# Loading wq in four strided quarters, x behind a tiny Exp, and a no-operation that waits for the last loads

## Chip, cores, metric

One core of a Trainium2 chip. The time is device time in microseconds (us) of one execution. Some executions here are about 1.2 to 1.6 us longer; they are called "slow" and left out of ratios. A ratio is the mean time of one kernel's fast runs over the mean of the other's fast runs of the same rounds on the same chip, so it is not quite the ratio of the medians that are quoted.

## The reference

A decode step for one token. `q = x @ wq` has 32 heads of 128; they attend to the last 4096 positions of 8 K/V heads, and the result goes through `wo`. Beside it stands a gated unit on the same x. A sigmoid gate mixes the two.

```python
q = (x @ wq).reshape(B, Sq, Hq, Dh).transpose(0, 2, 1, 3)      # x 1x512, wq 512x4096
k, v = k_cache[:, :, Sk - W:], v_cache[:, :, Sk - W:]           # 8 heads, W = 4096, Dh = 128
o = softmax(q @ k.T * Dh ** -0.5) @ v                           # k, v repeated over 4 heads each
a = o.reshape(B, Sq, Hq * Dh) @ wo                              # wo 4096x512
b = (sigmoid(x @ w_gate) * (x @ w_up)) @ w_down                 # F = 1792
g = sigmoid((x * gate_w).sum(-1, keepdims=True))
return g * a + (1 - g) * b
```

All of it is 30.67 MB of bf16 read once: a kernel of transfers.

## The kernel before

All large loads are issued by SyncE, in the order in which they are used, into tiles that are there from the start or come free on the way.

```python
const = ctx.enter_context(tc.tile_pool(name="const", bufs=1))
big = ctx.enter_context(tc.tile_pool(name="big", bufs=1))
blk = ctx.enter_context(tc.tile_pool(name="blk", bufs=4))
w14 = ctx.enter_context(tc.tile_pool(name="w14", bufs=3))
# ... cut: further pools
xr = const.tile([1, 2, D], BF16, name="xr")
nc.scalar.dma_start(xr[:, 0, :], A_x[0, :, :])
nc.scalar.dma_start(xr[:, 1, :], gate_w.rearrange("(o n) -> o n", o=1))

dq = nc.sync
wq_sb = big.tile([P, DC, HQ * DH], BF16, name="wq_sb", tag="big")
wq_v = A_wq.rearrange("(p c) n -> p c n", c=DC)      # 32 KB in a row for each of 128 partitions
dq.dma_start(wq_sb[:], wq_v)
# ... cut: K in 4 loads, w_gate, w_up (wx: a part of it, in 4 small loads), V in 4, wo in 2, w_down in 4
spare = const.tile([1, 1], F32, name="spare")
for _ in range(4):
    nc.vector.memset(spare[:], 0.0)
# ... cut: identities, x transposed by TensorE, the gate
for k in range(8):                                    # q: needs all partitions of wq
    # ... cut
    for c in range(DC):
        nc.tensor.matmul(q_ps[:], lhsT=xT[:, c:c + 1].to_broadcast([P, P]),
                         rhs=wq_sb[:, c, ks], start=(c == 0), stop=(c == DC - 1))
# ... cut: K transposed by VectorE, scores, softmax, V, gated unit, wo and w_down into a_ps, output
```

## Time and profile before

| | before |
|---|---|
| median of the first 3 runs (range) | 80.73 us (80.44 to 81.89) |
| span in the profile | 78.7 us |
| first packet of wq starts | 1.74 us |
| wq complete | 12.93 us |
| last piece of w_down complete | 75.84 us |
| output issued | 76.68 us |

"Complete" is the last increment of a load's semaphore, from the trace's records of increments; packets are from its records of DMA packets.

### The profile page before, as it was taken

How to read it: one execution, taken by the hardware profiler on the slowest of the kernel's cores; microseconds unless marked ns; L12 is line 12 of the kernel's file. 1: busy time of each engine (PE TensorE's matmuls, PEld its weight loads, DVE VectorE, ACT ScalarE, POOL GpSimd, SP SyncE). 2: the span in 40 equal slices, each digit the busy share in tenths (PEclk: the TensorE clock that was granted, in tenths of full speed). 3: DMA queues.
4: the chain of work that ended last, by engine and by line, in shares of the span. 5: the costliest groups of instructions: out<-in, count | busy, mean ns of one | idle time of the engine just before them, and what ended most of it. 6: DMA issues, size and time to landing. Idle time of an engine off the chain costs nothing.

```text
span 78.7 us, 798 instructions
## 1 busy us (share of the span) xinstructions
PE 52.5 (67%) x314; PEld 23.6 (30%) x314; DVE 38.8 (49%) x52; ACT 10.9 (14%) x20; POOL 3.3 (4%) x10
## 2 busy tenths in 40 slices
PE   0200094999905788898887307999996799567650
PEld 0200041344302333333332202344341345345420
DVE  1600920029869999999986349962000000690020
ACT  2400000247651000000002191000000002000010
POOL 7900000000000000000000000000000000000000
PEclk9999999999999999999999995699999999999997
DMA  7779799999999999999999999999999999999710
GB/s 184 300 316 533 316 483 391 408 425 458 441 408 416 425 474 416 386 437 417 438 410 426 441 416 441 408 433 441 416 433 433 424 425 433 416 391 409 290 42 1
DMA packets 2616, 30.71 MB, mean 390 GB/s; under 512 B 307, under 2 KB 438, under 8 KB 822
## 3 DMA queue, kind: packets, MB, share of 16 engines
q1 hardware_dynamic: 2608, 30.67, 92.9%
q8 instruction: 2, 0.03, 0.2%
q10 hardware_dynamic: 6, 0.00, 0.0%
HBM read 30.67 MB, written 0.00 MB: 390 GB/s over the span
## 4 chain that ended last, share of the span: by engine, by line
DMA 93%; SPq 2%; PE 1%; DVE 1%; issue 0%
DMA wd_sb<-in_B_w_down_dram 36%; DMA kn<-in_A_k_cache_dram 32%; DMA vv<-in_A_v_cache_dram 24%; SPq L84 2%; PE a_ps L290 1%; DVE res L341 1%; SPq L80 0%
## 5 line engine op out<-in xcount | busy, mean ns | idle before, releaser
L299 PE MATMUL pv_ps<-vv,eT 128*32 128x512 bf16 x64 | 15.9, 405 | 4.1 <-DVE eT L271 2.8
L227 PE MATMUL S_ps<-kT,qbig 128*128 128x512 bf16 x64 | 15.2, 378 | 5.0 <-DVE qbig L216 2.8
L188 DVE STREAM_TRANSPOSE kT<-kn 128x2048 f32<-128x2048 f32 x8 | 17.8, 2282 | 0.0
L227 PEld LDWEIGHTS <-qbig 128*128 128x128 bf16 x64 | 6.1, 97 | 14.1 <-issue 4.2
L299 PEld LDWEIGHTS <-eT 128*32 128x32 bf16 x64 | 6.2, 102 | 12.9 <-issue 4.2
L200 PE MATMUL q_ps<-wq_sb,xT 128*128 128x512 bf16 x32 | 8.8, 442 | 1.2 <-DMA wq_sb<-in_A_wq_dram 1.2
L318 DVE TENSOR_TENSOR oT<-o_ps,rb 128x32 bf16<-128x32 f32 x1 | 0.2, 191 | 13.5 <-PE o_ps L316 13.5
L205 DVE STREAM_TRANSPOSE qtT<-q_sb 128x512 f32<-128x512 f32 x4 | 2.7, 700 | 6.9 <-ACT q_sb L202 6.9
L182 PE MATMUL S_ps<-ident,other 2*128 2x512 bf16 x4 | 2.0, 611 | 5.8 <-DVE other L140 5.8
L202 ACT CAST q_sb<-q_ps 128x512 bf16<-128x512 f32 x8 | 4.7, 585 | 7.0 <-PE q_ps L200 7.0
L200 PEld LDWEIGHTS <-xT 128*128 128x128 bf16 x32 | 3.5, 111 | 6.8 <-issue 4.2
L290 PE MATMUL a_ps<-wo_sb,oY 128*1 128x256 bf16 x64 | 3.8, 272 | 1.5 <-DMA wo_sb<-in_A_wo_dram 1.2
L290 PEld LDWEIGHTS <-oY 128*1 128x1 bf16 x64 | 2.7, 83 | 3.1 <-issue 1.4
L271 DVE STREAM_TRANSPOSE eT<-e_sb 128x1024 bf16<-128x1024 bf16 x2 | 2.4, 1224 | 1.9 <-ACT e_sb L269 1.9
L254 ACT ACTIVATE sge<-gu_ps 128x448 f32<-128x448 f32 x1 | 0.5, 543 | 18.9 <-PE gu_ps L243 18.9
L309 ACT COPY pv_sb<-pv_ps 128x512 f32<-128x512 f32 x1 | 0.6, 585 | 17.7 <-PE pv_ps L299 17.7
L341 DVE CAST res<-a_ps 1x256 bf16<-1x256 f32 x1 | 0.4, 412 | 5.2 <-PE a_ps L290 5.2
L281 DVE RECIPROCAL sg<-sge 128x448 f32<-128x448 f32 x1 | 3.0, 2952 | 0.0
L165 DVE TENSOR_TENSOR gpr<-xr 1x512 f32<-1x512 bf16 x1 | 0.7, 679 | 4.6 <-DMA xr<-in_gate_w_dram 4.6
L249 DVE TENSOR_REDUCE pm<-S_ps 128x1 f32<-128x1024 f32 x2 | 2.4, 1208 | 0.9 <-PE S_ps L227 0.9
L290 PE MATMUL a_ps<-wd_sb,hT 128*1 128x256 bf16 x28 | 2.1, 271 | 0.8 <-DMA wd_sb<-in_B_w_down_dram 0.8
L148 PE MATMUL xt_ps<-ident,xr 1*128 1x1 bf16 x4 | 0.3, 165 | 3.5 <-POOL ident L126 3.5
(62 smaller groups left out, 31.0 us busy)
## 6 DMA issues: line engine op xcount, KB each, us to landing
kn<-in_A_k_cache_dram SPq DMA_DIRECT2D x4, 2048.0 KB, 27.2
vv<-in_A_v_cache_dram SPq DMA_DIRECT2D x4, 2048.0 KB, 19.1
wq_sb<-in_A_wq_dram SPq DMA_DIRECT2D x1, 4096.0 KB
wo_sb<-in_A_wo_dram SPq DMA_DIRECT2D x2, 2048.0 KB
wg_sb<-in_B_w_gate_dram SPq DMA_DIRECT2D x1, 1792.0 KB
wu_sb<-in_B_w_up_dram SPq DMA_DIRECT2D x1, 1456.0 KB
wd_sb<-in_B_w_down_dram SPq DMA_DIRECT2D x1, 1024.0 KB
wd_sb<-in_B_w_down_dram SPq DMA_DIRECT2D x1, 384.0 KB
```

The source lines that it names most:

```text
L84: dq.dma_start(t[:, n0:n1, :].rearrange("p n d -> p (n d)"), cache[0, 2 * a:2 * a + 2, SBASE:SBASE + W, :] .rearrange("y (x n) d -> x y n ...
L182: nc.tensor.matmul(S_ps[u // 2][:, u % 2, :], lhsT=other[:].rearrange("p o y u -> p (o y u)"), rhs=ident[0:2, 0:2].rearrange("p (o y) -> p ...
L188: nc.vector.transpose(t[:].bitcast(F32), kn[a][:, v * KB:(v + 1) * KB, :] .rearrange("p n d -> p (n d)").bitcast(F32))
L200: nc.tensor.matmul(q_ps[:], lhsT=xT[:, c:c + 1].to_broadcast([P, P]), rhs=wq_sb[:, c, ks], start=(c == 0), stop=(c == DC - 1))
L202: nc.scalar.copy(q_sb[:, ks], q_ps[:])
L205: nc.vector.transpose(qtT[:].bitcast(F32)[:, kq], q_sb[:].bitcast(F32)[:, kq])
L227: nc.tensor.matmul(S_ps[v][:, hb, :], lhsT=q_st[:, a, dhi, :, t], rhs=k_v[:, hb * 16:(hb + 1) * 16, dhi, :, t], start=False, stop=(a == HP ...
L249: nc.vector.tensor_reduce(pm2[:, v:v + 1], S_ps[v][:].rearrange("p a b -> p (a b)"), axis=AX.X, op=ALU.max)
L271: nc.vector.transpose(eT[:, :, v * KB:(v + 1) * KB, :].rearrange("p a n r -> p n a r"), e_sb[:, v, :].rearrange("p (n a r) -> p n a r", a= ...
L281: nc.vector.reciprocal(sg[:], sge[:])
L290: nc.tensor.matmul(a_ps[32 * i:32 * i + 1, i, 0:HN], lhsT=lhsT, rhs=rhs[:, i * HN:(i + 1) * HN], start=start, stop=stop)
L299: nc.tensor.matmul(pv_ps[32 * a:32 * a + 32, :, :], lhsT=eT[:, a, 4 * m:4 * m + 4, :].rearrange("p n r -> p (n r)"), rhs=vv[a][:, 4 * m:4 ...
```

## The change

The intent, as the diff lets one guess: to give wq the first place in the queues, to split it so that its first part is under way sooner while each part still touches every fourth partition, to fetch ScalarE's table early, and to have SyncE's waits for the loads done before the end.

```diff
+    ctx.enter_context(tc.manual_schedule(engines={mybir.EngineType.Activation}))
+    warm = const.tile([1, 1], F32, name="warm")
+    nc.vector.memset(warm[:], 0.0)
+    nc.scalar.activation(warm[:], warm[:], AF.Exp)
     xr = const.tile([1, 2, D], BF16, name="xr")
@@
-    dq.dma_start(wq_sb[:], wq_v)
+    for y in range(4):
+        dq.dma_start(wq_sb[y:P:4], wq_v[y:P:4])
@@ (the loads of K, V, wo and w_down are also kept in a list, loads)
+    seen = dq.nop()
+    for load in loads[-8:]:
+        tc.add_manual_dep(seen.ins, load.ins.name,
+                          mybir.DependencyInfo(mybir.DependencyClass.Sync, mybir.DependencyReason.DATA), reason="loads ended")
@@
-    for _ in range(4):
+    for _ in range(3):
         nc.vector.memset(spare[:], 0.0)
```

More of the change, by code (lines that the diff above doesn't have):

```diff
@@ L77 @@
     dq = nc.sync
+    loads = []
     wq_sb = big.tile([P, DC, HQ * DH], BF16, name="wq_sb", tag="big")
     wq_v = A_wq.rearrange("(p c) n -> p c n", c=DC)
-    dq.dma_start(wq_sb[:], wq_v)
+    for y in range(4):
+        dq.dma_start(wq_sb[y:P:4], wq_v[y:P:4])
     def load_pair(t, cache, a, n0=0, n1=NP):
-        dq.dma_start(t[:, n0:n1, :].rearrange("p n d -> p (n d)"),
-                     cache[0, 2 * a:2 * a + 2, SBASE:SBASE + W, :]
-                     .rearrange("y (x n) d -> x y n d", n=NP)[:, :, n0:n1, :].rearrange("x y n d -> x y (n d)"))
+        loads.append(dq.dma_start(t[:, n0:n1, :].rearrange("p n d -> p (n d)"),
+                                  cache[0, 2 * a:2 * a + 2, SBASE:SBASE + W, :]
+                                  .rearrange("y (x n) d -> x y n d", n=NP)[:, :, n0:n1, :].rearrange("x y n d -> x y (n d)")))
     kn = []
@@ L114 @@
     for c0 in (0, NC_O // 2):
-        dq.dma_start(wo_sb[:, c0:c0 + NC_O // 2, :], wo_v[:, c0:c0 + NC_O // 2, :])
+        loads.append(dq.dma_start(wo_sb[:, c0:c0 + NC_O // 2, :], wo_v[:, c0:c0 + NC_O // 2, :]))
     wd_sb = w14.tile([P, NJ, N_OUT], BF16, name="wd_sb", tag="w14")
@@ L119 @@
     for j0, j1 in zip(WD_SPLIT[:-1], WD_SPLIT[1:]):
-        dq.dma_start(wd_sb[:, j0:j1, :], wd_v[:, j0:j1, :])
+        loads.append(dq.dma_start(wd_sb[:, j0:j1, :], wd_v[:, j0:j1, :]))
+    seen = dq.nop()
+    for load in loads[-8:]:
+        tc.add_manual_dep(seen.ins, load.ins.name,
+                          mybir.DependencyInfo(mybir.DependencyClass.Sync, mybir.DependencyReason.DATA), reason="loads ended")
     identf = const.tile([P, P], F32, name="identf")
```

## The prediction

> **What bounds the kernel now.** I read the chain that ended last first, in order of time; its columns are start, duration, what.
>
> ```profile
> 2.52 25.10 DMA kn<-in_A_k_cache_dram
> ...
> 27.70 19.12 DMA vv<-in_A_v_cache_dram
> ...
> 46.84 28.67 DMA wd_sb<-in_B_w_down_dram
> 75.51 0.04 issue
> 75.55 0.66 PE a_ps L290 x6
> 76.20 0.40 DVE res L341
> ```
>
> From 2.5 to 75.5 us it is transfers only; compute adds about 1.1 us behind the last one. Then I asked whether the DMA queue ever runs dry, with the 40 slices and the queue table of the page (packets, MB, share of 16 engines):
>
> ```profile
> DMA  7779799999999999999999999999999999999710
> ...
> q1 hardware_dynamic: 2608, 30.67, 92.9%
> ```
>
> It is full from the fifth slice to the end, and only the first four slices (8 us) are ragged. The packet records of the trace say the same in detail: in the steady part a 32 KB packet takes 1.23 us on its DMA engine, so 16 engines move 16 x 32768 B / 1.23 us = 426 GB/s. 30.67 MB at that rate are 72.0 us. Transfers run from 1.74 us (first packet of wq) to 75.84 us (last increment of the last piece of w_down), 74.1 us. So all that could be won without moving fewer bytes is about 2.1 us, and it has two places. (a) The first packets of wq start between 1.74 and 2.55 us, end between 3.60 and 4.09 us, and take 1.4 to 2.15 us in place of 1.23. (b) At the end the 16 engines are not level: of the last load six increments come at 74.1 to 74.3 us, ten at 75.5 to 75.8 us. The change touches (a) alone.
>
> The start, from the timeline of the first 20 us (start, duration, engine, line; in brackets the idle time before and what ended it):
>
> ```profile
> 0.73 0.38 SPq L80 DMA_DIRECT2D wq_sb<-in_A_wq_dram  x1
> 0.74 0.51 ACTq L74 DMA_DIRECT2D xr<-in_A_x_dram  x1
> ...
> 1.28 0.21 ACTq L75 DMA_DIRECT2D xr<-in_gate_w_dram  x1
> ...
> 1.53 1.28 ACT L170 ACT_TABLE_LOAD   x1 [1.53 <-PEq L358]
> ...
> 7.83 0.68 DVE L165 TENSOR_TENSOR gpr<-xr 1x512 f32<-1x512 bf16 x1 [4.56 <-DMA xr<-in_gate_w_dram]
> ...
> 12.98 7.25 PE L200 MATMUL q_ps<-wq_sb,xT 128*128 128x512 bf16 x25 [1.17 <-DMA wq_sb<-in_A_wq_dram]
> ```
>
> The reader is to see that x and wq are issued at the same instant from two queues; that gate_w, issued 0.5 us later, is not usable before 7.8 us; and that the q matmuls wait for all of wq, until 12.98 us. Last, the slack of compute, from TensorE's timeline near the end:
>
> ```profile
> 61.58 2.97 PE L299 MATMUL pv_ps<-vv,eT 128*32 128x512 bf16 x13 [1.28 <-DMA vv<-in_A_v_cache_dram]
> ...
> 71.38 1.91 PE L290 MATMUL a_ps<-wo_sb,oY 128*1 128x256 bf16 x32 [1.22 <-DMA wo_sb<-in_A_wo_dram]
> ```
>
> TensorE waits 1.28 us for V and then 1.22 us for wo, then 0.61 and 0.19 us for w_down. Work that reaches TensorE up to about 1.28 + 1.22 = 2.5 us later than now still ends behind the same transfers.
>
> [...]
>
> **The change part by part.**
>
> *wq in four loads.* Same bytes, same 32 KB rows, eight packets per engine. SyncE pays four issues for one. An issue of 128 rows takes 0.38 us here, one of a single row 0.21 us, so I take 0.3 us for 32 rows, an estimate: about 1.2 us in place of 0.38, and the first K load is issued some 0.8 us later. That lies far ahead of need, since wq alone keeps the engines busy until 12.6 us. The eight completion semaphores are handed out in turn, so with three more loads the third K load must wait for the first quarter of wq, and the fourth for x; both come long before 12 us, while four to six MB are queued. Cost on the path: 0. The gain: in the old single load packets began over 0.8 us and none ended before 3.60. [...] The last of the old packets to begin still took 1.54 us, 0.31 over the steady 1.23, so of the mean excess (about 1.9 - 1.23 = 0.7 us) some 0.4 us can go. Every engine then ends 0.4 us earlier.
>
> *x and gate_w behind the Exp.* No instruction of ScalarE's arithmetic is saved on the path: the table load is in both kernels, and it was idle time before (the Exp that needs it runs at 10.5 us). The tiny Exp is about 0.2 us of an idle engine. Its purpose can only be to leave wq the first place. x is then issued at 1.0 us if the queue runs on beside the table load, at about 2.1 us if not. Behind wq's packets it will wait as gate_w does now: a landing at 6 to 8.5 us in place of 2.0, and gate_w at 8 to 11 in place of 7.8. VectorE does gpr, gsum, two small operations and xT after gate_w, 9.69 - 7.83 = about 1.9 us, and TensorE the four mask matmuls, 2.1 us. So q could begin at 13 to 15.2 us in place of 12.98, a delay of 0 to 2.2 us. VectorE's chain to the exponentials shifts by as much, and the slack of 2.5 us less the 0.4 us gained takes it up. Cost on the path: 0, probably.
>
> *The no-operation.* It is one wait more on a queue that has nothing to do; the waits at the end were there before:
>
> ```profile
> SPq L369 <- DMA wd_sb<-in_B_w_down_dram: 23.3, 3, 21.8
> ...
> SPq L369 <- DMA out_dram<-res: 1.1, 1, 1.1
> ```
>
> SyncE's final wait is for the output's landing at 77.77 us, 1.9 us after the last load. Five waits of some 20 to 30 ns and a branch fit in there. Cost 0. One memset fewer and one more on VectorE: 0.
>
> Sum: 0.4 us earlier, out of 80.7: 80.3 us.
>
> **The rivals.** [...] the quarters of wq could run as slowly as half rate: up to 9.8 us lost while wq is moving, and a time of 82 to 90 us. [...] Against it: the ordinary 128-row load shows no such conflict (1.23 us per packet on all 16), and the stride is what one would choose after seeing that it works. *The late x becomes the bound.* If gate_w lands later than 11.5 us, q starts after 15.5, slack is used up, and each further us costs one: 80.5 to 82. Against it: gate_w waits now for only four packets of 1.23 us. *Hidden anyway.* If the first packets are slow for another reason than their number (they all end within 0.5 us of each other whenever they began), the quarters save nothing: 80.7. I hold this nearly as likely as the gain. *A large gain* would need over 1.6 us; the whole excess of the start is 0.7 us, so only run-to-run scatter could show it.
>
> **Range and chances.** 80.3 is the gain of 0.4; nothing gained is 80.7, all 0.7 gained is 80.0, and three runs of the kernel before spread from 80.44 to 81.89. So 79.5 to 81.4. Faster by over 2% (below 79.1): 4%. Slower by over 2% (above 82.3)[...]: 11%. Within 2%: 85%.
>
> **What would show it.** Right: the first wq packets end near 3.4 us, wq is complete near 12.5, the last piece of w_down lands near 75.4, DMA slices stay full, q waits for x's chain instead of wq, yet TensorE still waits for V or wo near the end, and the time from the output's issue to the end is unchanged at about 2 us. Wrong: packets of wq of 2 us or more after the first, or wq complete after 14 us[...]; no wait of TensorE for V, wo or w_down at the end (late x); a dip in the DMA slices when SyncE waits for a quarter of wq (starved queue); a longer stretch after the output's issue (the no-operation).

## More of the kernel before

`const` is the first pool that is laid out in SBUF, and `big`, `blk` and `w14`, which hold the large tiles, follow it.

One more line of before is needed later, from the view of the instructions that touch wq's tile (ns minimum/median/maximum of an issue, first and last start):

```profile
L80 SPq DMA_DIRECT2D wq_sb<-in_A_wq_dram x1: 380/380/380, 0.7 to 0.7; - x1
```

SyncE spends 380 ns on the issue of 128 rows.

## The result

80.09 us median of 6 runs (80.03 to 81.62), where before has 80.65 us (80.44 to 81.89) in its 6. Ratio 0.9938, 95% interval 0.9917 to 0.9958: about half a microsecond, real and small. The number was predicted; where it comes from was not. First the chain that ended last, after (start, duration, what):

```profile
2.60 10.67 DMA wq_sb<-in_A_wq_dram
...
28.47 18.39 DMA vv<-in_A_v_cache_dram
...
46.88 28.30 DMA wd_sb<-in_B_w_down_dram
75.18 0.04 issue
75.22 0.66 PE a_ps L303 x6
75.88 0.40 DVE res L354
```

Compare the legs (the pieces of this chain) with those of before. The stream reaches the end of the first V load at the same time, 46.88 us against 46.84; the leg behind it takes 28.30 us in place of 28.67. The gain is 0.37 us in this leg, near the end, in loads that the change did not touch. At the start, where the prediction had it, there is a loss. The timeline of the first 20 us:

```profile
0.73 1.28 ACT L76 ACT_TABLE_LOAD   x1 [0.73 <-PEq L371]
...
0.73 2.52 SPq L87 DMA_DIRECT2D wq_sb<-in_A_wq_dram  x4
...
0.89 0.51 ACTq L78 DMA_DIRECT2D xr<-in_A_x_dram  x1
...
1.44 0.21 ACTq L79 DMA_DIRECT2D xr<-in_gate_w_dram  x1
...
5.83 0.68 DVE L178 TENSOR_TENSOR gpr<-xr 1x512 f32<-1x512 bf16 x1 [2.56 <-DMA xr<-in_gate_w_dram]
...
13.40 6.92 PE L213 MATMUL q_ps<-wq_sb,xT 128*128 128x512 bf16 x18 [3.59 <-DMA wq_sb<-in_A_wq_dram]
```

x is issued only 0.16 us later than before: ScalarE's queue runs on beside the table load (x issued at 0.89 us, the load from 0.73 to 2.01). The q matmuls still wait for wq and start at 13.40 us, 0.42 later. The view of wq's tile says why:

```profile
L87 SPq DMA_DIRECT2D wq_sb<-in_A_wq_dram x4: 556/581/657, 0.7 to 2.6; - x4
```

A strided load of 32 rows takes 556 to 657 ns to issue, more than the 380 ns of the single load of 128. The first packet of wq starts at 2.06 us (1.74 before), and wq is complete at 13.26 us (12.93). TensorE's waits near the end, from its timeline:

```profile
61.46 2.97 PE L312 MATMUL pv_ps<-vv,eT 128*32 128x512 bf16 x13 [0.31 <-DMA vv<-in_A_v_cache_dram]
...
71.19 1.91 PE L303 MATMUL a_ps<-wo_sb,oY 128*1 128x256 bf16 x32 [1.16 <-DMA wo_sb<-in_A_wo_dram]
73.64 2.19 PE L303 MATMUL a_ps<-wd_sb,hT 128*1 128x256 bf16 x28 [0.54 <-DMA wd_sb<-in_B_w_down_dram]
```

It still waits for V, wo and w_down, so the end is still a matter of transfers. The sum, by the increments: wq complete to the last piece of w_down complete is 75.84 - 12.93 = 62.91 us before and 75.52 - 13.26 = 62.26 us after. The stream is 0.65 us (1.0%) faster, its beginning 0.33 us later, and the end 0.32 us earlier. From the output's issue to the end of the span the profiles show 2.05 us in both.

What made the stream faster? Its packets are shorter: those of 16 KB that start between 42 and 72 us take 615.6 ns in the mean before (614 and 621 most often, 2 of 726 at 611) and 611 ns after (724 of 727; two that ran beside an instruction fetch took 1.1 us). The excess is not there from the start: before 24 us all 317 of the 16 KB packets of before take 611 ns, as after, and wq's 32 KB packets take 1213 ns most often in before and in p1_pad (below) alike. It sets in at about 25 us and stays to the end; why only then is not known. Nothing in the diff touches these loads, except where they land. `warm` is four bytes in the first pool, in a slot of 32, and it pushes every later tile up by 32 bytes. In the built programs wq's tile begins at byte 30432 of its partition before, 224 above a multiple of 256, and at 30464 = 119 x 256 after; K's and V's tiles at 63200 and at 63232 = 247 x 256; the other large tiles likewise. (The tiles in which the engines keep K transposed and their results move along; that the destinations of the loads are what counts is argued from the packets, and no run moves the one without the other.) So my theory (A) became: the gain is the alignment of the load destinations to 256 bytes, an accident of the tile `warm`. The rivals: Q, the quarters; X, x behind the Exp; N, the no-operation.

### The profile page after: what moved, and what is told of

Same layout as the page of the kernel before.

```text
span 78.4 us, 805 instructions
## 1 busy us (share of the span) xinstructions
PE 54.1 (69%) x314; PEld 24.0 (31%) x314; DVE 38.7 (49%) x52; ACT 11.1 (14%) x21; POOL 3.3 (4%) x10
## 4 chain that ended last, share of the span: by engine, by line
DMA 73%; PE 14%; DVE 6%; SPq 2%; ACT 1%; issue 1%
DMA wd_sb<-in_B_w_down_dram 36%; DMA vv<-in_A_v_cache_dram 23%; DMA wq_sb<-in_A_wq_dram 14%; PE q_ps L213 13%; DVE kT L201 3%; SPq L87 2%; DVE qbig L229 2%; DVE qtT L218 1%; PE a_ps L303 1%; ACT q_sb L215 1%; DVE res L354 1%
## 5 line engine op out<-in xcount | busy, mean ns | idle before, releaser
L240 PE MATMUL S_ps<-kT,qbig 128*128 128x512 bf16 x64 | 16.4, 409 | 3.8 <-DVE qbig L229 2.8
L312 PE MATMUL pv_ps<-vv,eT 128*32 128x512 bf16 x64 | 15.2, 411 | 3.1 <-DVE eT L284 2.8
L213 PE MATMUL q_ps<-wq_sb,xT 128*128 128x512 bf16 x32 | 9.9, 485 | 3.6 <-DMA wq_sb<-in_A_wq_dram 3.6
L282 ACT ACTIVATE e_sb<-S_ps,nb 128x1024 bf16<-128x1024 f32 x2 | 2.2, 1109 | 0.0
```

The source lines that it names most:

```text
L240: nc.tensor.matmul(S_ps[v][:, hb, :], lhsT=q_st[:, a, dhi, :, t], rhs=k_v[:, hb * 16:(hb + 1) * 16, dhi, :, t], start=False, stop=(a == HP ...
L282: nc.scalar.activation(e_sb[:, v, :], S_ps[v][:].rearrange("p a b -> p (a b)"), AF.Exp, bias=nb[:], scale=scale, accum_out=rs2[:, v:v + 1])
L312: nc.tensor.matmul(pv_ps[32 * a:32 * a + 32, :, :], lhsT=eT[:, a, 4 * m:4 * m + 4, :].rearrange("p n r -> p (n r)"), rhs=vv[a][:, 4 * m:4 ...
```

## The experiments

Twelve kernels. "Offset" is where the large tiles begin above a multiple of 256 bytes. The last two columns are from the profile, where that was of a fast run; the leg is the one of w_down in the chain that ended last, from the end of the first V load.

| run | offset | median us | ratio to before | 95% | wq complete | leg us |
|---|---|---|---|---|---|---|
| before | 224 | 80.65 | 1 | | 12.93 | 28.67 |
| changed kernel | 0 | 80.09 | 0.9938 | 0.9917 to 0.9958 | 13.26 | 28.30 |
| p1_pad | 0 | 79.84 | 0.9931 | 0.9915 to 0.9946 | 12.87 | 28.33 |
| q1_wq4 | 224 | 81.08 | 1.0082 | 1.0067 to 1.0097 | slow | slow |
| x1_exp | 224 | 80.58 | 1.0023 | 1.0002 to 1.0043 | 13.07 | 28.68 |
| n1_nop | 224 | 81.18 | 1.0011 | 0.9995 to 1.0027 | 13.05 | 28.66 |
| m1_after_off224 | 224 | 80.84 | 1.0029 | 1.0016 to 1.0043 | 13.27 | 28.67 |
| a1_after_one_wq | 0 | 80.44 | 0.9951 | 0.9903 to 0.9999 | slow | slow |
| pq_pad_wq4 | 0 | 80.40 | 0.9980 | 0.9967 to 0.9993 | 13.53 | 28.33 |
| qn_neighbours | 0 | 90.07 | 1.1173 | 1.1156 to 1.1190 | 23.44 | |
| o64_pad | 64 | 80.30 | 0.9980 | 0.9964 to 0.9996 | 12.92 | 28.61 |
| o128_pad | 128 | 80.29 | 0.9976 | 0.9960 to 0.9993 | 12.98 | 28.54 |
| pc_pad_cols | 0 | 80.41 | 0.9919 | 0.9903 to 0.9936 | 12.75 | 28.33 |
| px_pad_exp | 0 | 79.79 | 0.9918 | 0.9902 to 0.9934 | slow | slow |

Medians are over all runs of a kernel, slow ones too (three of six in n1_nop and pc_pad_cols), so the ratio is what to compare.

### p1_pad: the four bytes alone

```diff
+    pad0 = const.tile([1, 1], F32, name="pad0")
+    nc.vector.memset(pad0[:], 0.0)
     xr = const.tile([1, 2, D], BF16, name="xr")
@@
-    for _ in range(4):
+    for _ in range(3):
         nc.vector.memset(spare[:], 0.0)
```

> The kernel before with one more four-byte tile ahead of x's tile and nothing else; the large tiles then begin on a multiple of 256 bytes in their partition, as in the changed kernel, where before they began 32 bytes below one. Theory A (the four-byte tile of the Exp moved all load destinations, and aligned writes run about 1% faster): as fast as the changed kernel or faster, ratio 0.985 to 0.995, packets of 16 KB at 611 ns to the end, 4.85 us from one V load's landing to the next. Rival Q (the quarters of wq or their order make the gain): ratio 1.000, packets at 614 to 621 ns in the second half, 4.91 us.

Ratio 0.9931: the whole gain, from a tile that nothing reads. All 719 of the 16 KB packets that start between 42 and 72 us take 611 ns, and the leg in the chain is that of the changed kernel:

```profile
46.64 28.33 DMA wd_sb<-in_B_w_down_dram
```

Theory A holds here, and Q, X and N are not needed for the gain. (Nor is it the memset ahead of x: o64_pad and o128_pad below have it too.) (The spacing of the V loads was 4.84 to 4.89 us, where 4.85 was expected.)

### q1_wq4, x1_exp, n1_nop: each intended part alone, addresses as before

```diff
 q1_wq4
-    dq.dma_start(wq_sb[:], wq_v)
+    for y in range(4):
+        dq.dma_start(wq_sb[y:P:4], wq_v[y:P:4])
 x1_exp (the operand shares the tile spare, so that no large tile moves; the small ones of the first pool do, by 32 bytes)
+    spare = const.tile([1, 2], F32, name="spare")
+    nc.vector.memset(spare[:, 0:1], 0.0)
+    nc.scalar.activation(spare[:, 0:1], spare[:, 0:1], AF.Exp)
     xr = const.tile([1, 2, D], BF16, name="xr")
 n1_nop
+    seen = dq.nop()      # and the eight dependencies of the change
```

> The kernel before with wq in four loads alone; addresses as before. Theory A: no gain, and the later first packets cost 0.2 to 0.4 us, ratio 1.002 to 1.006, wq complete near 13.2 us. Rival Q: the whole gain, ratio 0.992 to 0.995.

> The kernel before with x and gate_w behind the tiny Exp alone, its operand kept in a tile that is there anyway, so that the addresses of the large tiles stay as before. Theory A: within 0.2% of before. Rival X (freeing the first moments of the transfer queue makes the gain): 0.992 to 0.995, and wq's first packets earlier than 1.74 us.

> The kernel before with the no-operation of SyncE alone. Theory A: within 0.2% of before, the time from the output's issue to the end unchanged at 2.05 us. Rival N (the waits done ahead of the end make the gain): 0.992 to 0.995, with a shorter stretch after the output's issue.

None gains. The quarters cost 0.8%, more than the 0.2 to 0.6% that I expected. The Exp costs 0.2%, barely clear of nothing, and the no-operation nothing that can be seen. Rivals Q, X and N all fail as causes of the gain. (What the no-operation does beside the quarters is another matter; see pq_pad_wq4.) In x1_exp the first packet of wq starts at 1.74 us as before: with wq in one load, x's place makes no difference to when wq begins.

### m1_after_off224: the changed kernel, its alignment taken away

```diff
     (the changed kernel)
+    pad0 = const.tile([1, 56], F32, name="pad0")      # 224 bytes
+    nc.vector.memset(pad0[:, 0:1], 0.0)
     xr = const.tile([1, 2, D], BF16, name="xr")
```

> The changed kernel with 224 bytes more ahead of x's tile, so that its large tiles begin 32 bytes below a multiple of 256 again, as in the kernel before; all three intended parts are in. Theory A (alignment is the whole gain): the gain is gone, ratio to the kernel before 1.000 to 1.012 (1.001 if the gain of alignment is 0.7% here as in the padded kernel, up to 1.012 if the costs measured for the parts alone add up), packets of 16 KB at 614 to 621 ns in the second half. Rival: some of the gain comes from the parts together: ratio under 0.998.

Ratio 1.0029: with all three parts in and the alignment gone the kernel is slower than before. Its leg is that of before again:

```profile
47.15 28.67 DMA wd_sb<-in_B_w_down_dram
```

p1_pad shows that the alignment suffices, m1_after_off224 that the gain is gone without it. The three parts together cost about 0.3%, less than the sum of their costs alone (0.82 + 0.23 + 0.11 = 1.16%); part of the difference is explained under pq_pad_wq4.

### a1_after_one_wq and pq_pad_wq4: the quarters among aligned tiles

```diff
 a1_after_one_wq (from the changed kernel)
-    for y in range(4):
-        dq.dma_start(wq_sb[y:P:4], wq_v[y:P:4])
+    dq.dma_start(wq_sb[:], wq_v)
 pq_pad_wq4: p1_pad with the quarters of the change
```

> The changed kernel with wq in one load again, aligned, x behind the Exp and the no-operation kept. If the quarters only cost (first packet 0.3 us later): faster than the changed kernel, ratio to before 0.988 to 0.991, wq complete by 12.9 us. If the quarters help beside the other two parts: slower than the changed kernel, 0.995 or more.

> The padded kernel with wq in four loads, x issued first as before, no no-operation. If the cost of the quarters (0.8% alone) is the same with aligned tiles: ratio to before 1.000 to 1.003. If it is a property of the unaligned kernel: 0.993 to 0.996. Then x behind the Exp would be what the changed kernel needs the first case for.

a1_after_one_wq is inconclusive: of its four fast runs three took 79.74 to 79.99 us and one 80.89, and the interval reaches from 0.990 to 1.000. (The run of 80.89 us lies nearer to its slow ones, 81.12 and 81.20; without it the ratio would be 0.992, but that is a choice made after the fact.)

pq_pad_wq4 came out between its two cases: with aligned tiles and x issued first the quarters cost 0.998 - 0.993 = 0.5%, and this padded kernel is slower than the changed one (0.9980 against 0.9938, or 0.34 us), which differs from it in x's place and the no-operation. The end of the traces shows where much of that lies. From the output's issue to the end of the span pq_pad_wq4 takes 2.29 us, and so do the two other kernels with four loads of wq and no no-operation (q1_wq4 2.29, pc_pad_cols 2.30); the other eleven take 2.05 to 2.07 us. SyncE's own waits in pq_pad_wq4 have this line, where before had 1.1 us for the output and 23.3 us for w_down:

```profile
SPq L372 <- DMA out_dram<-res: 25.4, 1, 25.4
```

Before, SyncE waits for the loads first and for the output last. Here the long wait at the end is the one for the output, and four waits on loads that landed long ago are still made behind it, 62 to 67 ns apart, where before has one. In the changed kernel the no-operation has made these waits earlier. So the no-operation, which gains nothing alone, seems to take back the 0.24 us that the quarters add at the end; what changes the order of the waits is argued: the three loads more shift the semaphores that later transfers get (in the traces the transfers take eight in turn, and the output has number 110 before and 104 in the changed kernel). The rest of the 0.34 us may be x's place behind the Exp: the last of the first 16 packets ends at 4.63 us with x first and at 4.38 us in the changed kernel, and wq is complete at 13.53 and 13.26 us. No run isolates either part beside the quarters.

### qn_neighbours: quarters of 32 neighbouring partitions

```diff
-        dq.dma_start(wq_sb[y:P:4], wq_v[y:P:4])
+        dq.dma_start(wq_sb[32 * y:32 * y + 32], wq_v[32 * y:32 * y + 32])
```

> The changed kernel with the quarters of wq made of 32 neighbouring partitions in place of every fourth. [...] packets of wq near 2.4 us in place of 1.22, wq complete near 20 us, ratio to before 1.05 to 1.10. Rival (the choice of partitions does not matter): packets 1.22 us, ratio as the changed kernel, 0.99 to 0.995. In either case the issue shows whether its 0.56 us came from the stride: near 0.38 us or less if so.

Ratio 1.117, 9.5 us over before. wq's packets take 2.56 us in the median in place of 1.22, and the row of GB/s in the page's 40 slices (2.2 us each) shows the first nine or so at about half rate:

```profile
GB/s 133 222 134 222 238 237 237 237 208 82 311 467 430 408 467 415 415 459 390 447 432 427 400 454 445 400 459 422 415 459 408 437 452 408 437 422 389 356 108 0
```

TensorE's timeline has the price:

```profile
23.58 8.94 PE L213 MATMUL q_ps<-wq_sb,xT 128*128 128x512 bf16 x32 [6.34 <-DMA wq_sb<-in_A_wq_dram]
```

The expected time of wq was near 20 us, from 2.4 us a packet, a guess that no run had shown; it was 23.4. So which partitions one load spans matters very much here: 2.56 us a packet with 32 neighbours, 1.22 us with every fourth partition. The prediction's first rival had half rate for the quarters; why neighbours are slow is not shown. The view of wq's tile settles the issue time as well:

```profile
L87 SPq DMA_DIRECT2D wq_sb<-in_A_wq_dram x4: 383/409/789, 0.7 to 2.1; - x4
```

The first issue takes 383 ns here and its first packet starts at 1.75 us: the 556 ns and the start at 2.06 us of the changed kernel belong to the stride, not to the number of loads.

### o64_pad and o128_pad: how much alignment is needed

```diff
 o64_pad: in p1_pad, const.tile([1, 24], ...); o128_pad: const.tile([1, 40], ...)
```

> The kernel before with 96 bytes ahead of x's tile: large tiles begin 64 bytes above a multiple of 256. If a write must begin on a multiple of 256 bytes to run at the better rate: as before, ratio 0.998 to 1.003, 16 KB packets at 614 to 621 ns in the second half. If a multiple of 64 is enough: as the padded kernel, 0.991 to 0.995, 611 ns.

> The kernel before with 160 bytes ahead of x's tile: large tiles begin 128 bytes above a multiple of 256. If only multiples of 256 count: ratio 0.998 to 1.003. If 128 is enough: 0.991 to 0.995 and 611 ns.

Most of the gain is gone at 64 and at 128. The leg of o64_pad, then that of o128_pad:

```profile
46.70 28.61 DMA wd_sb<-in_B_w_down_dram
```

```profile
46.81 28.54 DMA wd_sb<-in_B_w_down_dram
```

Of the 0.34 us between the worst and the best alignment (28.67 and 28.33) they win 0.06 and 0.13. Both ratios, 0.9980 and 0.9976, lie at the lower edge of what was expected for "only 256 counts" (the second just outside) and away from "as the padded kernel". Of the four offsets tried (0, 64, 128 and 224) only 0 has the full gain; others were not tried.

### pc_pad_cols and px_pad_exp: candidates

```diff
 pc_pad_cols (from p1_pad)
-    dq.dma_start(wq_sb[:], wq_v)
+    for c in range(DC):
+        dq.dma_start(wq_sb[:, c, :], wq_v[:, c, :])
 px_pad_exp: the change's warm, memset and Exp alone, in their own tile
```

> A candidate to beat both: the padded kernel with wq in four loads by column block, each of 128 partitions and 8 KB rows[...]. If smaller first packets shorten the slow start: ratio to before 0.985 to 0.990. If the slow start is a fixed delay of about 0.7 us: as the padded kernel, 0.991 to 0.996.

> The kernel before with x and gate_w behind the tiny Exp in a tile of its own, as in the changed kernel, which also aligns the large tiles; wq in one load, no no-operation. If alignment is all: as the padded kernel, 0.991 to 0.995. If x behind the Exp helps the start too: under 0.991; if it costs as it seemed to in the unaligned kernel (0.2%): 0.994 to 0.997.

0.9919 and 0.9918, both as the padded kernel within their intervals. With 8 KB packets the first 16 end at 2.1 to 2.9 us, but wq is complete at 12.75 us, only 0.12 ahead of the padded kernel's: smaller first packets hardly shorten the slow start. At the output's issue pc_pad_cols is 0.28 us ahead of p1_pad (75.84 against 76.12 us), but its end takes 0.23 us longer (2.30 against 2.07, see pq_pad_wq4). With the no-operation it might gain these 0.23 us, 0.3%: an estimate from the two traces, and not run. Apart from the inconclusive a1_after_one_wq, the aligned versions that load wq over all partitions at once stand at 0.992 to 0.993 and the changed kernel at 0.994; these differences are not resolved, so none is shown to beat the changed kernel. p1_pad does as well as the changed kernel with none of its three parts.

## Why the prediction was right in its number and wrong in its reason

It said 80.3 us, 79.5 to 81.4, and within 2%: 80.09 us was measured. Step by step:

- *What bounds the kernel.* Right: a full transfer queue to the end, TensorE waiting for V, wo and w_down before and after. Its bound on the gain, "about 2.1 us" in two places, was not right: it took 426 GB/s, from 1.23 us for a packet of 32 KB, for a fixed rate. The records of before have 1.213 us in the median for these packets (432 GB/s) and 611 ns for those of 16 KB until 24 us (429 GB/s); behind that packets took 0.8% longer, and this excess could be won. Nothing in the prediction asked for that.
- *"Every engine then ends 0.4 us earlier"*, from the quarters. Wrong, in sign too: this is the step that failed. That a smaller load starts sooner was my assumption; no trace of before showed it. The first packets end at 3.91 to 4.38 us where 3.60 to 4.09 stood and near 3.4 was forecast, wq is complete 0.33 us later, and q1_wq4 alone costs 0.8%. The issue of 32 strided rows was estimated at 0.3 us from the rows' number; it takes 0.56 us, because of the stride (qn_neighbours). Its own lines spoke against a rule by rows: x, a single row, took 0.51 us to issue. The "Cost on the path: 0" of the four loads also missed the end: without the no-operation they lengthen it by 0.24 us (2.29 against 2.05).
- *"One memset fewer and one more on VectorE: 0."* The memset is free, but its tile is the gain: 0.65 us in the stream (0.50 in p1_pad: 75.28 - 12.87 = 62.41 us against 62.91). The sum lacked this term. It could have been found beforehand: the built program has every tile's address, and the order of instructions, which I did look at, does not show it.
- *x and gate_w late.* Wrong. x was usable at 2.3 us (2.0 before, 6 to 8.5 foreseen), gate_w at 5.8 (7.8 before, 8 to 11 foreseen): hardly later, and earlier. With wq issued in four slow pieces there was probably less in the queue ahead of them: in x1_exp, with wq in one load, x's last increment comes at 5.39 us and gate_w's at 7.86 us, against 7.81 before. q therefore waited for wq and not for x. That it would be hidden was right.
- *The no-operation.* Right as to its cost: 1.0011 alone, and 2.05 us from output to end before and after. That these 2.05 us would be 2.29 with the quarters and without it was not seen.
- *The first rival, the quarters at half rate.* A guess that no trace of before showed. It did not occur with every fourth partition (1.22 us a packet), and with neighbouring ones it is real: 2.56 us a packet and 9.5 us in qn_neighbours, against the bound of 9.8 us that was given. By what mechanism is not shown.
- *Rival "hidden anyway".* Nearest to the truth about the intended parts, which won nothing over the kernel before.

A gain of 0.56 us in the medians was thus forecast as 0.4 by a term that measured the other way, beside one that was not in the sum. That the number fell into the range was luck and is no support for the reasoning.

## What to carry to other kernels

Where a kernel is bound by its loads, look at the byte at which each large tile begins in its partition: here a start on a multiple of 256 took about 1% off the stream (0.50 to 0.65 of 62.9 us, most of it after about 25 us), and one small tile ahead of it decided that. When a change that adds or removes a tile moves the time a little, compare the addresses and run a control that moves them alone, and one that puts them back, before crediting the intended parts. Split loads only so that each part still spans the same spread of partitions (here 1.22 us a packet with every fourth partition, 2.56 us with 32 neighbours), measure what a strided form costs to issue (0.56 us here, against 0.38), and look at what the added loads do to the waits at the end (2.29 us from the output's issue to the end, against 2.05).

## What the runs measured of the loads

- Large load destinations at 224 bytes above a multiple of 256 cost 0.7% of the kernel, and offsets 64 and 128 still 0.5% (legs of 28.67, 28.61 and 28.54 us against 28.33 us aligned).
- Unaligned 16 KB packets between 42 and 72 us took 615.6 ns in the mean against 611 ns, 0.8%, and the leg 28.67 us against 28.33 us, 1.2%; but before 24 us all 317 unaligned packets of 16 KB took 611 ns. The mechanism is not shown.
- In loads from SyncE's queue quarters of 32 neighbours had packets of 2.56 us, of every fourth partition 1.22 us. A strided quarter of 32 partitions kept the full rate here (1.22 us a packet, against 1.21 us in the load of 128).
- The issue of a load depended on its stride: 556 ns for 32 strided partitions, 383 ns for 32 neighbouring ones, 380 ns for 128, and the first packet 0.3 us later with the stride (2.06 us against 1.75 and 1.74).
- Observed, not tested: in the profiles that fell in the slow state (q1_wq4, a1_after_one_wq and px_pad_exp), one increment of the 16 of the first V load comes 1.0 to 1.6 us behind the 15th, and two of the last load's are late, where in before and after the last nine or ten end within 0.4 us.
